# Which engine copies the probability tiles out of the matmul banks: from two engines to one, with the first output columns of two head pairs copied together

## The chip, the cores and the metric

The kernel runs on one core of a Trainium2 chip. The metric is the device time of one execution in microseconds (us). The kernel before took 426.64 us, the median of three runs (426.52, 426.64 and 428.88). The execution that was profiled took 426.48 us. Its trace spans 424.8 us, so 1.7 us lie outside of what the rows below can show.

## The reference

The inputs are q, k and v of shape 8 batches x 8 heads x 576 tokens x 64, and f, one forget value per batch, head and token. First comes a causal attention with a decay, then a small expert layer on the tokens of each batch with the highest scores:

```
scores = scale * q @ k^T                       # scale = 1/8
cum    = cumsum(log(clip(f, 1e-4, 1)))
scores = where(causal, -1e9, scores + cum_q - cum_k)
attn   = exp(scores - max);  attn = attn / (sum + 1e-9)
x      = (attn @ v), heads side by side        # 8 x 576 x 512
for each batch b:
    top = the 128 tokens with the highest x[b] @ w_gate
    xe  = x[b, top]
    out[b, top] = xe + sigmoid(xe @ w_gate) * (relu(xe @ w1) @ w2)
    out[b, others] = x[b, others]
```

Everything is float32. w1 is 512 x 1024 and w2 is 1024 x 512.

## The kernel before, in words

**Work by pairs of heads.** There are 32 pairs, four per batch. `pair_ops(p)` loads a pair's q and k and, per head, the decay row `e`, from which GpSimd cuts causal masks `m` (line 438). `pair_parts(p)` is the rest of a pair:

- TensorE computes the scores of the pair in four groups into PSUM banks (line 606). These matmuls use 64 rows of the array, since the heads are 64 wide, and two heads run side by side.
- VectorE adds mask or decay, writes the result to `p` and keeps the row minimum `nm` (line 650).
- ScalarE takes the exponential of `p` in place and sums the rows (line 698).
- TensorE transposes `p` in blocks of 64 columns into a pair of banks (line 717), in four groups: block row 3, then 1, 2 and 0.
- The transposed probabilities are copied from the banks into the tile `pt`, one copy per head and group. `copy_on` does it on ScalarE (line 351) or VectorE (line 355). The choice is the flag `other`: the second head's copy of the groups 2 and 3 goes to VectorE, all others to ScalarE. These two groups are the widest, 384 and 512 columns per head.
- TensorE multiplies `v` with `pt` (line 800; called the product below). The first 128 query columns of a pair go to one bank, the other 448 to a second. An even pair and the odd pair behind it share the first bank, side by side.
- The product is copied to a tile `ot` in two copies, 128 and 448 columns (line 351), transposed back (line 859), and VectorE scales it into `x` (line 864). `ot` has two buffers, so that a pair is turned back while the next is being copied.

**The expert layer by batches.** GpSimd forms the gate scores of a pair as soon as its `x` is there (lines 873, 877). With four pairs done, the scores of the batch are ranked on VectorE (line 1005), the 128 tokens gathered by DMA (line 1046), transposed (line 1068), multiplied with w1 (lines 1117, 1124) and w2 (lines 1170, 1178), and scattered back (line 1189). These matmuls use all 128 rows of the array; they are called MLP matmuls below. Each weight is split in two parts, high and low, for accuracy, mostly on GpSimd (lines 934, 937).

**What sets the order.** The program is not written in the order in which it runs. The class `Flow` is a planner: each step is added with the engine or engines that may do it, a cost, the steps it comes after, the buffers it takes and gives, and a number `place`. The planner then walks through modelled time and issues on each engine the ready step with the smallest place. The places are sums of constants (BD, PL, PM, PC and so on). Tokens named "ps" are the eight PSUM banks; others stand for tile buffers. For a step that either of two engines may do, BD is a handicap on VectorE, and with it the product's copies all went to ScalarE. Each engine executes its own instructions strictly in the order that the planner gave.

The functions that the diff touches:

Of the kernel before, what the change touches and what calls it, by code (L numbers as in the profile page):

```python
# [8 lines left out]
F32 = mybir.dt.float32  # L9
# [9 lines left out]
P = 128  # L19
# [12 lines left out]
class Flow:  # L32
# [16 lines left out]
           ("long", "full"): 0.02, ("full", "long"): 0.08,  # L49
           ("av", "row"): 0.15, ("av", "turn"): 0.13, ("av", "long"): 0.12, ("av", "full"): 0.1,  # L50
           ("row", "av"): 0.13, ("turn", "av"): 0.16, ("long", "av"): 0.2, ("full", "av"): 0.1}
# [127 lines left out]
def kernel(  # L179
# [32 lines left out]

    BD = 13.742
    WP = 17
    WQ = 0
    R0 = -128.692
    X0 = -110.557
    XE_ = -374.815
    XH_ = 10.943
    XM_ = -139.592  # L220
    XB_ = -7.064
    XN_ = -144.178
    XO_ = -217.739
    XU_ = 1.221
    XQ_ = 1037.015
    XR_ = 452.972
    XG_ = 100.433
    PL4 = -197.666
    GW = 62.808
    EPS = 0.124  # L230
    LOOK = 13
    PR = -556.913
    PL = -142.848
    PS = 1725.901
    PV = 96.032
    PM = -87.342
    PE_ = 464.517
    PC = -268.952
    PB = -64.844
    PD = -22.685  # L240
    VO = -0.967
    VD = 1
    GD = 0.1
    WS = -60.896
    WD = 742.816
    WL = 434.464
    RK = 76.029
    RD = -1.849
    XP = 18.421
    GO = 35.674  # L250
    GS = 0.497
    GL = 28.239
    LG = 2.69
# [49 lines left out]
    sgs = [const.tile([P, NCH], F32, name=f"sg{r}") for r in range(2)]  # L303

    vrs = [const.tile([P, NCH, P], F32, name=f"v{r}") for r in range(3)]
    ptb = [const.tile([P, 5 * 640], F32, name=f"pt{r}") for r in range(2)]
# [33 lines left out]
    def act(n):  # L340
        return {"act": n / 1200 + 0.05}
# [7 lines left out]
    def copy_on(e, d, s_):  # L349
# [4 lines left out]
        else:  # L354
            nc.vector.tensor_copy(d, s_)  # L355

    flow = Flow({"raw": 3, "rq": 3, "v": 3, "p0": 2, "p1": 2, "p4": 2, "pt": 2, "ot": 2,
                 "x": 2, "nm": 10, "h": 1, "hth": 1, "htl": 1, "xth": 1, "xtl": 1, "xe": 2, "srow": 1,
# [8 lines left out]
    z = {}  # L367
# [8 lines left out]
    def t_ones(e):  # L376
        z["ones"] = work.tile([P, S], F32, tag="ot", name="ones", bufs=2)
        nc.vector.memset(z["ones"], 1.0)
# [12 lines left out]

    tk_h, tk_ot, tk_srow = Token("h"), Token("ot", 3), Token("srow")
    tk_ep = Token("hth")
# [158 lines left out]
    NT = 4  # L552
    vts, pts, ots, xhs = {}, {}, {}, {}
    gates = {b: {"tk": Token("gs"), "done": []} for b in range(B)}
# [4 lines left out]
    def pair_parts(p):  # L559
# [148 lines left out]
        for i in (3, 1, 2, 0):  # L708
# [53 lines left out]
            for hh in range(2):  # L762
                other = hh == 1 and i >= 2
                if i == 0:
                    n_ = 4 * P - 2 * R * hh
                    x6 = add({"dve": n_ / 960 + 0.13} if other else {"act": n_ / 1200 + 0.1}, lambda e, cps=cps, hh=hh: cps(e, hh), after=[x5, d_rows],
                             place=t + PC + 0.01 * hh, give=[tk_t])
                else:
                    x6 = add(dve(2 * w) if other else act(2 * w), lambda e, cp=cp, hh=hh: cp(e, hh=hh), after=[x5, d_rows],
                             place=t + PC + 0.01 * hh, give=[tk_t])  # L770
                copied.append(x6)
# [5 lines left out]
        pieces = ((0, 1), (1, 1), (0, 0), (2, 1), (4, 1), (3, 1))  # L777
        tk_ot = Token("ot", 1)
        if odd:
            tk_av = [tails[p - 1], Token("ps")]  # L780
        else:

            tk_av = [Token("ps", 2), Token("ps")]
            tails[p] = tk_av[0]
        wdone = []
        avs = []
        for n, (j, g) in enumerate(pieces):
# [3 lines left out]
            def av(e, n=n, j=j, g=g, q0=q0, q1=q1):  # L791
                if j == 0:
                    avb[p, g] = bank(tk_av[g])
                if n == 0:
                    ots[p] = work.tile([P, S], F32, tag="ot", name=f"ot{p}", bufs=2)
                vt, pt = vts[p], pts[p]
                qo = SPL if odd and g == 0 else 0
                for par in range(2):
                    off = (640 * j if par == 0 else 2624 - 512 * j) + q0 - j * P
                    nc.tensor.matmul(  # L800
                        avb[p, g][par * D:(par + 1) * D, qo + q0 - g * SPL:qo + q1 - g * SPL],
                        vt[:, j, par * D:(par + 1) * D], pt[:, off:off + q1 - q0],
                        start=(j == 0), stop=(g == 0 or n == len(pieces) - 1))
# [3 lines left out]
        def av_all(e):  # L807
            for fn, _ in avs:
# [6 lines left out]
                 place=at + 0.01 * odd, take=[tk_ot] + tk_av[odd:], give=[tk_pt, tk_v], kind="av", lat=0.05)  # L815
        for g, w in ((0, SPL), (1, S - SPL)):
            def out(e, g=g, w=w):
                qo = SPL if odd and g == 0 else 0
                copy_on(e, ots[p][:, g * SPL:g * SPL + w], avb[p, g][:, qo:qo + w])

            avd[p] = x5
            wdone.append(add({**act(w), **dve(w)}, out, after=[x5], place=at + 0.2 + 0.3 * odd, give=[tk_av[g]]))

        rn = rns[b % 2][:, :, 2 * hp:2 * hp + 2]

# [26 lines left out]
        def back(e):  # L852
            ot = ots[p]
            tb = st["tb"] = pair(tk_b)
# [412 lines left out]
```

## Time and profile before

| | kernel before |
|---|---|
| median of three runs | 426.64 us |
| profiled execution, and its span | 426.48 us, 424.8 us |
| TensorE (PE) busy | 381.4 us, 90% |
| VectorE (DVE) busy | 307.7 us, 72% |
| ScalarE (ACT) busy | 306.7 us, 72% |
| GpSimd (POOL) busy | 262.9 us, 62% |
| VectorE's probability copies (line 355) | 64, 39.3 us |
| ScalarE's probability copies (line 351, into `pt`) | 256 |
| mean DMA rate | 162 GB/s |

Busy time is a share of the whole span, and the span has several stages: a short start, a stretch of attention alone, a long stretch in which attention and MLP matmuls mix, and an end with MLP matmuls alone. Which engine limits a stage must be read from that stage. A wait in the profile is idle time of an engine before an instruction, put down to what released it last.

### The profile page before, as it was taken

What the parts mean: (1) busy time and instruction counts of PE and PEld (TensorE: products, weight loads), DVE (VectorE), ACT (ScalarE), POOL (GpSimd) and SP (SyncE); (2) the same over time, 40 slices, a digit from 0 to 9 for tenths busy, and PEclk for the clock granted to TensorE, in tenths of its full rate; (3) what the DMA queues carried; (4) which work ended last, traced back from release to release, by engine and by line L of the source; (5) the groups of instructions that cost most, each with busy time, mean ns of one, the idle gap of its engine ahead of it and who ended that gap; (6) DMA issues with size and microseconds to landing.
All of it is one profiled execution on the core that took longest, in us unless ns stands there. A gap on an engine that the chain in (4) does not pass through costs nothing. (4 is left out here: it accounts for less than half of the span.)

```text
span 424.8 us, 11756 instructions
## 1 busy us (share of the span) xinstructions
PE 381.4 (90%) x3897; PEld 270.6 (64%) x3897; DVE 307.7 (72%) x1079; ACT 306.7 (72%) x961; POOL 262.9 (62%) x412
## 2 busy tenths in 40 slices
PE   2889998998979899989899999899989999999995
PEld 1546656566556657566576767668576766868873
DVE  5658758785989899869696976978689685825421
ACT  2887999898898998766787777966888767513220
POOL 5585779997959889766483665547574654134201
PEclk9898999999999999999999999999999999999999
DMA  7798977876979787563576637726674423011101
GB/s 167 198 235 208 258 212 222 228 225 169 282 175 249 200 234 220 169 176 104 157 193 168 183 113 198 232 70 175 206 193 131 139 60 95 17 50 57 49 2 49
DMA packets 77155, 68.67 MB, mean 162 GB/s; under 512 B 47747, under 2 KB 56998, under 8 KB 77094
## 3 DMA queue, kind: packets, MB, share of 16 engines
q1 hardware_dynamic: 75654, 63.43, 54.5%
q0 software_dynamic: 1280, 4.20, 3.1%
q8 instruction: 31, 0.51, 0.6%
q14 instruction: 30, 0.25, 0.2%
q10 hardware_dynamic: 160, 0.30, 0.2%
HBM read 56.18 MB, written 11.70 MB: 160 GB/s over the span
## 5 line engine op out<-in xcount | busy, mean ns | idle before, releaser
L698 ACT ACTIVATE p<-p,nm 128x448 f32<-128x448 f32 (+4 forms) x288 | 165.9, 582 | 9.9 <-DVE nm L650 9.6
L438 POOL TENSOR_SCALAR_AFFINE_SELECT m<-e 128x320 f32<-128x320 f32 (+3 forms) x256 | 114.3, 476 | 45.5 <-DMA e<-eq 16.4
L606 PE MATMUL banks<-rk,rq 64*128 64x192 f32 (+4 forms) x768 | 120.5, 427 | 13.0 <-DMA rq<-in_qk_dram 8.4
L351 ACT COPY pt<-banks 128x256 f32<-128x256 f32 (+4 forms) x256 | 91.2, 400 | 21.6 <-DVE pt L355 10.0
L650 DVE CUSTOM_DVE_ANT_0 p<-banks,m 128x320 f32<-128x320 f32 (+3 forms) x256 | 100.6, 418 | 6.7 <-PE banks L606 3.5
L606 PEld LDWEIGHTS banks<-rk,rq 64*128 64x128 f32 x768 | 74.3, 193 | 34.3 <-DVE nm L650 9.8
L800 PE MATMUL banks<-pt,v 128*64 128x448 f32 (+4 forms) x768 | 91.7, 391 | 0.2
L717 PE MATMUL banks<-ident,p 64*128 64x64 f32 x1472 | 69.6, 226 | 15.5 <-DVE pt L355 9.9
L717 PEld LDWEIGHTS banks<-ident,p 64*128 64x128 f32 x1472 | 61.8, 139 | 27.3 <-DVE pt L355 14.3
L800 PEld LDWEIGHTS banks<-pt,v 128*64 128x64 f32 x768 | 48.1, 137 | 45.5 <-issue 29.9
L355 DVE COPY pt<-banks 128x512 f32<-128x512 f32 x64 | 39.3, 622 | 27.8 <-ACT pt L351 20.5
L873 POOL TENSOR_TENSOR gj<-x,wg 128x640 f32<-128x640 f32 x24 | 37.4, 1558 | 33.3 <-DVE x L864 33.1
L698 ACT ACTIVATION_READ_ACCUMULATOR p<-p,nm 128x1 f32 x288 | 55.6, 193 | 0.0
L864 DVE TENSOR_TENSOR x<-banks,rn 128x640 f32<-128x640 f32 x32 | 26.3, 820 | 25.6 <-PE banks L859 24.5
L351 ACT COPY ot<-banks 128x128 f32<-128x128 f32 x64 | 22.4, 404 | 30.2 <-PE banks L800 29.8
L877 POOL TENSOR_TENSOR acc<-acc,gj 128x640 f32<-128x640 f32 x24 | 38.3, 1596 | 1.6
L1005 DVE SCALAR_TENSOR_TENSOR j<-srow,sg,later 128x576 uint8<-128x576 f32 (+1 forms) x40 | 35.9, 898 | 0.7
L1189 POOL DMA_INDIRECT out_dram<-xe,idx x8 | 8.6, 1080 | 43.9 <-DVE xe L1185 27.5
L650 DVE CUSTOM_DVE_ANT_0 p<-banks,e 128x384 f32<-128x384 f32 x64 | 34.7, 548 | 0.4
L650 DVE CUSTOM_DVE_ANT_0 p<-banks,m,nm 128x192 f32<-128x192 f32 x64 | 26.6, 415 | 8.4 <-ACT p L698 2.7
L650 DVE DVE_READ_ACCUMULATOR2_ANT nm<- 128x1 f32 (+1 forms) x384 | 31.0, 81 | 0.0
L1170 PE MATMUL banks<-w2h,hth 128*128 128x512 f32 x64 | 25.9, 405 | 0.5 <-ACT hth L1150 0.3
(83 smaller groups left out, 415.9 us busy)
## 6 DMA issues: line engine op xcount, KB each, us to landing
e<-eq SPq DMA_DIRECT2D x62, 288.0 KB
rk<-in_qk_dram SPq DMA_DIRECT2D x32, 288.0 KB
out_dram<-x SPq DMA_DIRECT2D x16, 512.0 KB
rq<-in_qk_dram SPq DMA_DIRECT2D x32, 144.0 KB
rq<-in_qk_dram SPq DMA_DIRECT2D x32, 128.0 KB
v<-in_v_dram SPq DMA_DIRECT2D x32, 128.0 KB
v<-in_v_dram SPq DMA_DIRECT2D x32, 80.0 KB
srow<-sd SPq DMA_DIRECT2D x7, 320.0 KB
```

Source lines behind the costliest of these rows:

```text
L351: nc.scalar.copy(d, s_)
L355: nc.vector.tensor_copy(d, s_)
L438: nc.gpsimd.affine_select(out=dst, in_=src, pattern=w, compare_op=ALU.is_ge, fill=NEG, base=base, channel_multiplier=1)
L606: nc.tensor.matmul(st["sc", u][hh][:, o:o + k1 - k0], q_rows(raws["q", p], hh, i), raws["k", p][rows, k0:k1], start=True, stop=True)
L650: nc.vector.tensor_tensor_reduce(out=into(hh, i, r_, x0, x1), in0=blocks(b_[r_, x0 - k0:x1 - k0], hh, i), in1=blocks(in1(), hh, i), scale= ...
L698: nc.scalar.activation(x, x, AF.Exp, bias=st["nm", hh, i], scale=-1.0, accum_out=l)
L717: nc.tensor.transpose(tp[:, g, col:col + R], src, ident[g * R:g * R + R, g * R:g * R + R])
L800: nc.tensor.matmul(avb[p, g][par * D:(par + 1) * D, qo + q0 - g * SPL:qo + q1 - g * SPL], vt[:, j, par * D:(par + 1) * D], pt[:, off:off + ...
L864: nc.vector.tensor_tensor(out=xhs[key][:, :, w_ * P:(w_ + 1) * P].rearrange("p c (h d) -> p c h d", h=2), in0=st["tb"][:, :, 0:NCH * D].re ...
L873: nc.gpsimd.tensor_tensor(out=gj if hp else acc, in0=xhs[key][:, :, w0:w1], in1=wg[:, hb * HB + w0:hb * HB + w1].unsqueeze(1).broadcast_to ...
L877: nc.gpsimd.tensor_tensor(out=acc, in0=acc, in1=gj, op=ALU.add)
L1005: nc.vector.scalar_tensor_tensor(junk[0:n, :], st["srow"][0:n, 0:S], sg()[0:n, c:c + 1], later[0:n, o:o + S], ALU.subtract, ALU.is_gt, acc ...
```

## The change

Five things are different.

- `other` is always false: the 64 probability copies of VectorE are ScalarE's now.
- The two output buffers become one tile `both`, 128 x 2 x 576, one half for even pairs and one for odd.
- The 448 columns of each pair are still copied after that pair's product. The first 128 columns of an even pair are no longer copied on their own: after the odd pair's product one copy takes both pairs' columns from the shared bank (`heads`).
- The rest of a pair (`back_parts`: row sums, turning back, scaling, gate) is added after that joint copy for both pairs, so an even pair is turned back only when the odd pair's product is there.
- The planner has a cost between two products in a row, ("av", "av"), and nearly all its constants have new values, so that nearly every engine's instructions stand in another order.

```diff
-           ("av", "row"): 0.15, ("av", "turn"): 0.13, ("av", "long"): 0.12, ("av", "full"): 0.1,
+           ("av", "row"): 0.15, ("av", "turn"): 0.13, ("av", "long"): 0.12, ("av", "full"): 0.1, ("av", "av"): 0.15,
...
-    BD = 13.742
+    BD = 17.003
...
-    EPS = 0.124
+    EPS = 0.061
...
+    both = const.tile([P, 2, S], F32, name="both")
...
-    flow = Flow({"raw": 3, "rq": 3, "v": 3, "p0": 2, "p1": 2, "p4": 2, "pt": 2, "ot": 2,
+    flow = Flow({"raw": 3, "rq": 3, "v": 3, "p0": 2, "p1": 2, "p4": 2, "pt": 2, "ot0": 1, "ot1": 1,
...
-                other = hh == 1 and i >= 2
+                other = False
...
-        tk_ot = Token("ot", 1)
+        tk_ot = Token(f"ot{odd}")
...
-            tk_av = [Token("ps", 2), Token("ps")]
+            tk_av = [Token("ps"), Token("ps")]
...
-        for g, w in ((0, SPL), (1, S - SPL)):
-            def out(e, g=g, w=w):
-                qo = SPL if odd and g == 0 else 0
-                copy_on(e, ots[p][:, g * SPL:g * SPL + w], avb[p, g][:, qo:qo + w])
-
-            avd[p] = x5
-            wdone.append(add({**act(w), **dve(w)}, out, after=[x5], place=at + 0.2 + 0.3 * odd, give=[tk_av[g]]))
-
+        def out(e):
+            copy_on(e, both[:, odd, SPL:S], avb[p, 1][:, 0:S - SPL])
+
+        def heads(e):
+            copy_on(e, both[:, :, 0:SPL], avb[p, 0][:, 0:2 * SPL].rearrange("p (g x) -> p g x", g=2))
+
+        avd[p] = x5
+        wdone.append(add(act(S - SPL), out, after=[x5], place=at + 0.2 + 0.3 * odd, give=[tk_av[1]]))
+        if odd:
+            x5 = add(act(2 * SPL), heads, after=[x5], place=at + 0.2 + 0.3 * odd, give=[tk_av[0]])
+            rests[p - 1](x5)
+            back_parts(p, st, wdone, at, sums, d_l, tk_ot, x5)
+        else:
+            rests[p] = lambda x: back_parts(p, st, wdone, at, sums, d_l, tk_ot, x)
+
+    def back_parts(p, st, wdone, at, sums, d_l, tk_ot, joint):
+        b, hp = divmod(p, NP)
+        odd = p % 2
+        wdone = wdone + [joint]
...
-            ot = ots[p]
+            ot = both[:, odd, :]
```

How the change moves instructions is shown at three places. The first is ScalarE's order around the copies of pair 13 (`pt1` is the probability tile of odd pairs, `p13` and `p14` hold the exponentials of pairs 13 and 14, `nm` their row minima). Before:

```order
L698 ACTIVATE p13_2_2271,st1_100<-p13_2_2271,nm13_3_1_2483 128x192
L351 COPY pt1_114<-banks_78 128x4x128
L351 COPY pt1_114<-banks_78 128x2x128 x2
L698 ACTIVATE p14_0_2460,st2_101<-p14_0_2460,nm14_0_0_2485 128x576
L351 COPY pt1_114<-banks_78 128x3x128
```

And now:

```order
L352 COPY pt1_115<-banks_78 128x4x128 x2
L699 ACTIVATE p13_2_2350,st1_100<-p13_2_2350,nm13_3_1_2421 128x192
L352 COPY pt1_115<-banks_78 128x2x128 x2
L699 ACTIVATE p14_0_2529,st2_101<-p14_0_2529,nm14_0_0_2549 128x576
L352 COPY pt1_115<-banks_78 128x3x128 x2
```

The 128x4x128 and 128x3x128 copies, of which ScalarE had one each, stand there twice in a row. Over the whole program ScalarE's probability copies go from 256 to 320 and VectorE's from 64 to none.

The second place is ScalarE's order around the output copies of pairs 10 and 11. Before:

```order
L351 COPY ot10_2284<-banks_78 128x128
L351 COPY ot10_2284<-banks_78 128x448
L698 ACTIVATE p40_97,st0_99<-p40_97,nm12_3_0_2251 128x64
L698 ACTIVATE p12_2_2217,st0_99<-p12_2_2217,nm12_3_1_2269 128x192
L698 ACTIVATE p13_0_2244,st1_100<-p13_0_2244,nm13_0_1_2343 128x576
L351 COPY ot11_2323<-banks_78 128x128
L351 COPY ot11_2323<-banks_78 128x448
```

And now, from pair 11's copies on (pair 10's 128x448 stands 17 rows higher):

```order
L352 COPY pt0_114<-banks_78 128x2x128 x2
L352 COPY both_110<-banks_78 128x448
L352 COPY both_110<-banks_78 128x2x128
L699 ACTIVATE p13_2_2350,st1_100<-p13_2_2350,nm13_3_0_2412 128x192
L699 ACTIVATE p13_0_2297,st1_100<-p13_0_2297,nm13_1_1_2360 128x320
```

One 128x2x128 copy stands where each pair had its own 128x128.

The third place is TensorE's order where the MLP matmuls begin (`xth0` is the first batch's gathered tokens, `w1h` and `w1l` the two parts of w1). Before, with the products of pairs 12 and 13 just ahead of these rows:

```order
L717 MATMUL banks_78<-ident_81,p14_0_2460 128x64
L606 MATMUL banks_78<-rk15_2260,rq0_86 128x64 x2
L606 MATMUL banks_78<-rk15_2260,rq0_86 128x192 x2
L606 MATMUL banks_78<-rk16_2556,rq1_87 128x384 x2
L606 MATMUL banks_78<-rk16_2556,rq1_87 128x192 x2
L606 MATMUL banks_78<-rk16_2556,rq1_87 128x320 x2
L717 MATMUL banks_78<-ident_81,p15_0_2597 128x64 x24
L1117 MATMUL banks_78<-w1h_115,xth0_0_2759 128x512
L1117 MATMUL banks_78<-w1l_116,xth0_0_2759 128x512
L1117 MATMUL banks_78<-w1h_115,xth0_0_2759 128x512
L1117 MATMUL banks_78<-w1l_116,xth0_0_2759 128x512
```

And now, with pair 10's product just ahead:

```order
L607 MATMUL banks_78<-rk13_1866,rq1_87 128x384 x2
L1127 MATMUL banks_78<-w1h_116,xth0_0_2292 128x512
L1127 MATMUL banks_78<-w1l_117,xth0_0_2292 128x512
L607 MATMUL banks_78<-rk13_1866,rq1_87 128x192 x2
L607 MATMUL banks_78<-rk13_1866,rq1_87 128x320 x2
L718 MATMUL banks_78<-ident_81,p12_0_2087 128x64 x16
L607 MATMUL banks_78<-rk13_1866,rq1_87 128x448 x2
L799 MATMUL banks_78<-pt1_115,v2_113 64x448 x4
```

The first MLP matmul comes after 11 products instead of 14, and the MLP matmuls stand in pieces between attention steps instead of in one block. Counted over the whole program, TensorE's order passes from steps with a 64-row contraction (scores, transposes of `p` and of outputs) to steps that use 128 rows (MLP matmuls, products, index steps) 33 times before and 58 times now. The number of its instructions is the same. The first 27 rows of SP's queue (its loads) are the same, and so is TensorE's order behind the product of pair 31, but for the turns back of pairs 30 and 31 and the last batch's score rows, which stand a few MLP matmuls later.

## Rows read from the trace of the kernel before

**Rows 1.** The page, part 1: busy us (share of the span) xinstructions

```profile
PE 381.4 (90%) x3897; PEld 270.6 (64%) x3897; DVE 307.7 (72%) x1079; ACT 306.7 (72%) x961; POOL 262.9 (62%) x412
```

**Rows 2.** Windows: stretch, its length, busy time of each engine, granted clock, DMA

```profile
20.00:140.00 120.00, 107.45 (x1278) 71.43 (x1275) 93.13 (x364) 106.66 (x353) 96.78 (x151) 0.98 0.81 223
134.00:164.00 30.00, 26.91 (x367) 18.82 (x363) 26.76 (x90) 26.65 (x91) 26.32 (x38) 1.00 0.78 198
164.00:375.00 211.00, 198.41 (x2037) 143.16 (x2038) 163.86 (x566) 156.79 (x493) 121.91 (x185) 1.00 0.52 148
```

**Rows 3.** Waits: who waited for whom, total us, times, longest us

```profile
DVE pt L355 <- ACT pt L351: 20.5, 29, 3.0
...
ACT pt L351 <- DVE pt L355: 10.0, 18, 1.0
PE banks L717 <- DVE pt L355: 9.9, 15, 1.3
...
PE banks L859 <- ACT ot L351: 5.0, 7, 0.9
...
PE banks L717 <- ACT pt L351: 2.6, 5, 1.2
```

**Rows 4.** Lines by shape, ScalarE: busy us, mean ns, idle before

```profile
L351 ACT COPY pt<-banks 128x256 f32<-128x256 f32 x96 | 32.6, 377 | 3.2 <-PE banks L717 2.7
...
L351 ACT COPY pt<-banks 128x512 f32<-128x512 f32 x32 | 18.8, 588 | 5.8 <-PE banks L717 4.2 <-DVE pt L355 1.5
...
L351 ACT COPY pt<-banks 128x384 f32<-128x384 f32 x32 | 15.5, 484 | 10.0 <-DVE pt L355 8.5 <-PE banks L717 1.5
...
L351 ACT COPY ot<-banks 128x128 f32<-128x128 f32 x32 | 8.5, 266 | 29.8 <-PE banks L800 29.8
```

**Rows 5.** Lines by shape, VectorE: the probability copies

```profile
L355 DVE COPY pt<-banks 128x512 f32<-128x512 f32 x32 | 22.1, 691 | 17.0 <-ACT pt L351 14.3 <-PE banks L717 2.7
L355 DVE COPY pt<-banks 128x384 f32<-128x384 f32 x32 | 17.7, 553 | 10.8 <-ACT pt L351 6.2 <-PE banks L717 4.3
```

**Rows 6.** Windows of line 355 alone: stretch, length, VectorE busy (x instructions)

```profile
20.00:140.00 120.00, 14.86 (x24) 0.98 0.81 223
```

**Rows 7.** Timeline of all engines from 105.5: start, length, engine, line, operation

```profile
105.82 1.11 ACT L351 COPY pt<-banks 128x512 f32<-128x512 f32 x3
...
106.42 0.69 DVE L355 COPY pt<-banks 128x512 f32<-128x512 f32 x1 [0.34 <-ACT pt L351]
...
107.16 0.14 PEld L717 LDWEIGHTS banks<-ident,p 64*128 64x128 f32 x2 [0.73 <-DVE pt L355]
```

**Rows 8.** Timeline of TensorE, 128 to 166, the last stretch without MLP matmuls

```profile
131.67 5.62 PE L800 MATMUL banks<-pt,v 128*64 128x448 f32 x48
...
150.60 5.62 PE L800 MATMUL banks<-pt,v 128*64 128x448 f32 x48
...
163.96 0.50 PE L1117 MATMUL banks<-w1h,xth 128*128 128x512 f32 x1
164.29 0.39 PE L1117 MATMUL banks<-w1l,xth 128*128 128x512 f32 x1
```

**Rows 9.** Timeline of TensorE, 183 to 200

```profile
195.58 1.20 PE L1178 MATMUL banks<-w2h,htl 128*128 128x512 f32 x4 [0.42 <-DVE g L1089]
196.71 1.34 PE L717 MATMUL banks<-ident,p 64*128 64x64 f32 x36
```

**Rows 10.** Timeline of TensorE, the end

```profile
404.60 0.46 PE L1068 MATMUL banks<-ident,xe 64*128 64x64 f32 x8
...
406.04 0.39 PE L1117 MATMUL banks<-w1h,xth 128*128 128x512 f32 x1
...
411.50 1.07 PE L1178 MATMUL banks<-w2h,htl 128*128 128x512 f32 x4
412.41 1.03 PE L1143 MATMUL banks<-ident,h 128*128 128x128 f32 x8
```

More of the change, by code (lines that the diff above doesn't have):

```diff
@@ L211 @@
     FR = 3 * R
-    BD = 13.742
+    BD = 17.003
     WP = 17
     WQ = 0
[L216 to L229, printed above, removed]
-    EPS = 0.124
-    LOOK = 13
[L232 to L241, printed above, removed]
+    R0 = -112.531
+    X0 = -80.055
+    XE_ = -435.953
+    XH_ = 35.944
+    XM_ = -269.256
+    XB_ = -6.162
+    XN_ = -260.971
+    XO_ = -297.011
+    XU_ = 1.451
+    XQ_ = 887.605
+    XR_ = 440.833
+    XG_ = 122.837
+    PL4 = -306.718
+    GW = 70.696
+    EPS = 0.061
+    LOOK = 13
+    PR = -444.931
+    PL = -62.883
+    PS = 1660.693
+    PV = 149.607
+    PM = -69.055
+    PE_ = 360.879
+    PC = -267.606
+    PB = -34.433
+    PD = -18.932
+    VO = -1.905
     VD = 1
     GD = 0.1
[L244 to L252, printed above, removed]
+    WS = -90.032
+    WD = 727.705
+    WL = 447.716
+    RK = 69.243
+    RD = -2.401
+    XP = 25.102
+    GO = 33.367
+    GS = 0.817
+    GL = 22.573
     LG = 2.69
@@ L376, in t_ones @@
     def t_ones(e):
-        z["ones"] = work.tile([P, S], F32, tag="ot", name="ones", bufs=2)
+        z["ones"] = both[:, 0, :]
         nc.vector.memset(z["ones"], 1.0)
@@ L390, in t_ec @@
         nc.vector.tensor_scalar(z["ec"], z["cum"], -8.0, None, ALU.mult)
-    tk_h, tk_ot, tk_srow = Token("h"), Token("ot", 3), Token("srow")
+    tk_h, tk_ot, tk_srow = Token("h"), Token("ot0", 3), Token("srow")
     tk_ep = Token("hth")
@@ L552 @@
     NT = 4
-    vts, pts, ots, xhs = {}, {}, {}, {}
+    vts, pts, xhs, rests = {}, {}, {}, {}
     gates = {b: {"tk": Token("gs"), "done": []} for b in range(B)}
@@ L793, in av @@
                     avb[p, g] = bank(tk_av[g])
-                if n == 0:
-                    ots[p] = work.tile([P, S], F32, tag="ot", name=f"ot{p}", bufs=2)
                 vt, pt = vts[p], pts[p]
```

## The prediction, made before the changed kernel was run

> **What bounds the kernel now.** I read the busy times first. TensorE is busy for 381.4 us of 424.8, VectorE and ScalarE for about 307 each [rows 1]. So TensorE is nearest to its limit, and a change that leaves its work alone can only win or lose its idle time, 43.4 us in all, or change what it costs to pass from one kind of step to another. The windows tell where that idle time lies [rows 2]. From 20 to 140, where there is attention alone, TensorE is busy for 107.45 of 120 and ScalarE for 106.66: two engines at 89%, each with about 13 us to spare. From 164 to 375, with MLP matmuls mixed in, TensorE has 198.41 of 211, ScalarE only 156.79. There TensorE alone sets the pace. The attention stretch moves two pairs in 18.93 us (products at 131.67 and 150.60 [rows 8]).
>
> The waits come next [rows 3]. TensorE's transposes wait 9.9 us, 15 times, for a copy on VectorE to free their banks, 2.6 us for copies on ScalarE, and its turns back 5.0 us for output copies. VectorE's own copies stand waiting for ScalarE's copies for 20.5 us, ScalarE's for VectorE's for 10.0 us: the two write the same tile and go one behind the other. The timeline shows such a pair of copies [rows 7]: ScalarE's 128x512 copy starts at 105.82, VectorE waits 0.34 us and starts at 106.42, and the weight load of the next transposes has waited 0.73 us when the copy releases it at 107.16.
>
> **The change, part by part.** The sum is made against the profiled 426.48 us, 0.16 below the median of 426.64.
>
> *Copies leave VectorE.* 32 of 691 ns and 32 of 553 ns go, 39.8 us with their 27.8 us of idle time in front [rows 5]. VectorE is not the limit (307.7 of 424.8), so this counts only through who waits for it. On ScalarE such copies take 588 and 484 ns [rows 4], so the second of a pair ends a little over 0.1 us earlier, and the hand-over falls away; in exchange it stands in a fuller queue. Of the 9.9 us of TensorE's waits I take half as gained: **-5.0**. The ends are 0 (each wait is replaced by one for ScalarE) and -9.9.
>
> *ScalarE's load.* It gets 32 x 588 + 32 x 484 ns = 34.3 us more. The joint copy takes 377 ns by the row of 128x256, instead of 2 x 266 [rows 4]: 16 x 155 ns = 2.5 us less. In sum 306.7 + 31.8 = 338.5, 80% of the span. What matters is the attention stretch. Of the 64 copies 24 lie there, 14.86 us on VectorE [rows 6]; at ScalarE's durations, 12 of each width, they are 12.9, less 6 x 0.155 for the joint copies: 106.66 + 12.0 = 118.7 of 120. That would be full. It is a little less in fact, since copies in a row overlap (the three at 105.82 take 1.11 us together [rows 7], their durations of 588, 377 and 377 add to 1.34), and a third of ScalarE's 10.0 us of waits for VectorE, 3.3, should lie in this stretch and go. If only that gives way, the stretch grows by 12.0 - 3.3 = 8.7; if its other 10 us of idle time closes too, by 0. Since TensorE has as much slack there as ScalarE, and VectorE delivers its minima sooner, I take **+1.5**.
>
> A rule speaks against this step. The Trainium skill, page "TensorEngine Tiling (Array Packing)", section "PSUM Bottleneck", says that where tiling has made the matmuls quick, copies out of PSUM may become the limit, and to use both ScalarE and VectorE for them. By that rule the term would be the upper end, +8.7, and the change a loss; the windows, with 54 us of ScalarE's time free behind 164, bear it out for the first stretch alone.
>
> *MLP matmuls three pairs earlier.* They begin after 11 products instead of 14. Before, they start at 163.96 [rows 8]; from 134 to 164 TensorE is idle for 3.1 us of 30 [rows 2], and now there is work to lay in. I take **-2.5** (ends 0 and -3.1).
>
> *MLP matmuls in pieces.* From 164 to 375 TensorE is idle for 12.6 us [rows 2]. About half of the 9.9 us is part of it and already counted; of the other 8 or so I take a third as filled by pieces: **-2.5** (ends 0 and -8).
>
> *More passages.* TensorE passes from 64-row to 128-row steps 58 times instead of 33. The price: four MLP matmuls inside a block take 0.91 us from start to start (411.50 to 412.41 [rows 10]), four that stand alone between a wait and transposes 1.13 (195.58 to 196.71 [rows 9]), 0.22 more for going in and out. At the first passage, 163.96, the first matmul takes 0.33 to the second's start [rows 8], 0.10 more than the usual 0.23, which agrees. 25 x 0.22 = **+5.5**. The ends are 0, if every piece lies in time that was idle, and 12.5, if each costs a whole first matmul of 0.50.
>
> *The joint copy.* An even pair's turn back now waits for the odd pair's product. Behind it stand scaling and gate, which have most of a pair's time to spare; the token of `both` is given back before the next even product, a pair later. I cost it at nothing, with what that rests on: an odd pair's product, copy and turns back keep ahead of the next even pair's. Its cost without that cover is the third rival.
>
> *Start and end.* SP's first loads are the same, and the first matmul waits for them. At the end the last batch's gathered tokens are transposed at 404.60 and needed at 406.04 [rows 10]: 1.4 us of slack take the later turns back of pairs 30 and 31, about one copy of 0.54 and two MLP matmuls. Both at 0.
>
> Sum: -5.0 + 1.5 - 2.5 - 2.5 + 5.5 = -3.0, so **423.5 us**, 0.7% below the median. That is within the 1% (4.3 us) that a measurement of this kernel can tell from no change.
>
> **The rivals.** *VectorE's copies were the whole trouble.* All of the 9.9 and 3.1 go, the filling gives 2.5, and half of the passages fall into idle time (+2.75): 426.5 - 12.75 = 413.7. For it: VectorE loses 67 us of copies and waits, and minima, ranks and scaling all come sooner. Against: the copies still come one after the other.
>
> *ScalarE becomes the bound of the attention stretch.* It stands in the place of VectorE in the waits (0 instead of -5.0), its stretch grows by 8.7, passages cost 5.5, and only the -5.0 of the two MLP terms and half a gain of 2.5 remain: 426.5 + 6.7 = 433.2. It decides where ScalarE's share from 20 to 140 passes about 95% and exponentials queue behind copies. For it: 118.7 of 120. Against: the MLP matmuls now start inside that stretch, so a slow ScalarE no longer leaves TensorE without work.
>
> *The joint copy holds up the turns back.* TensorE already waits 5.0 us for output copies [rows 3]. Each of 16 times the odd product is followed by a 448 copy and a joint one, and turns back for two pairs behind them. If half of these cost 0.6 us, that is 4.8 more: 428.3.
>
> That the copies don't move can be left out: the order has none on VectorE.
>
> **How the numbers follow.** Forecast 0.42, its own range 419 to 428; VectorE the whole trouble 0.28; ScalarE the bound 0.20; joint copy 0.10. Faster by over 1% means below 422.4: all of the second and a quarter of the first, 0.39. Slower by over 1% means above 430.9: nearly all of the third case and little of others, 0.20. The rest, 0.41, is within 1%. With a tenth left out on each side the range is 414 to 434.
>
> **What would show it.** VectorE's busy time near 268 and no copy of `pt` on it. ScalarE's near 335, and its share from 20 to 140 above 95%: if TensorE's idle time in that stretch stays near 12, my +1.5 holds; if it grows beyond 18, the second rival does. TensorE's waits of transposes for copies in sum near 7.5 instead of 12.5. The first MLP matmul near 140. TensorE's busy time up by some 4 to 6 for the passages; if it stays at 381, that term was too large. Turns back waiting much more than 5.0 would be the third rival. I am wrong altogether if the time is far from 423.5 and TensorE's idle time and passages don't account for it, for instance by a later start or a gap at the end.

## The result, and the profile after

The changed kernel takes 413.79 us, the median of four runs (412.55 to 415.16); the kernel before took 426.72 in the same comparison (426.52 to 428.88). The ratio is 0.9687, with a 95% interval from 0.9643 to 0.973: 3.1% faster. The forecast was 423.5, and the range ended at 414, just above the measured time. The number of the first rival, 413.7, came out, though its mechanism accounts for a part only, as the experiments show.

The profiled execution took 413.60 us, its span is 411.9. Part 1 of the page, busy us (share of the span) xinstructions, answers to [rows 1]:

```profile
PE 384.9 (93%) x3897; PEld 269.0 (65%) x3897; DVE 269.5 (65%) x1015; ACT 328.4 (80%) x1009; POOL 260.6 (63%) x412
```

TensorE's busy time rose by 3.5 us, and its idle time fell from 424.8 - 381.4 = 43.4 to 411.9 - 384.9 = 27.0, by 16.4. The span fell by 12.9, the difference of the two. So the whole gain is idle time of TensorE. The windows say where it was. First the kernel before, in three stretches that [rows 2] do not have (length, busy time of PE, PEld, DVE, ACT, POOL with their instructions, granted clock, DMA share, GB/s):

```profile
8.40:31.00 22.60, 19.23 (x166) 12.34 (x168) 15.28 (x56) 18.19 (x53) 13.13 (x26) 0.92 0.82 208
31.00:140.00 109.00, 98.41 (x1164) 65.88 (x1161) 87.24 (x338) 97.09 (x321) 88.24 (x137) 0.98 0.80 220
140.00:375.00 235.00, 219.59 (x2318) 158.15 (x2314) 184.96 (x641) 178.48 (x565) 143.35 (x216) 1.00 0.55 154
```

The same stretches of the changed kernel, and two that answer to [rows 2]:

```profile
8.40:31.00 22.60, 19.43 (x164) 13.74 (x166) 14.41 (x55) 19.22 (x54) 13.96 (x28) 0.85 0.78 220
20.00:140.00 120.00, 112.54 (x1281) 73.41 (x1281) 82.86 (x348) 114.46 (x372) 100.04 (x156) 0.96 0.83 225
31.00:140.00 109.00, 102.06 (x1169) 66.43 (x1167) 77.27 (x322) 104.42 (x340) 90.73 (x140) 0.97 0.82 222
...
164.00:375.00 211.00, 209.41 (x2167) 148.96 (x2166) 140.91 (x539) 174.66 (x536) 123.67 (x187) 1.00 0.53 152
140.00:375.00 235.00, 232.09 (x2422) 164.03 (x2418) 160.32 (x598) 195.44 (x601) 145.32 (x215) 1.00 0.55 157
```

TensorE's idle time from 31 to 140 goes from 10.59 to 6.94, from 140 to 375 from 15.41 to 2.91. These are 3.65 and 12.50, nearly all of the 16.4. From 8.4 to 31, and in what lies outside 8.4 to 375, next to nothing changed (3.4 and 3.2; 14.0 in both). From 164 to 375 TensorE is busy for 209.41 of 211 us. In that stretch only 1.6 us of waits are left that another order could remove. (A busy TensorE is not TensorE at its peak: its matmuls overlap in the trace, so short stalls can lie inside busy time.)

Its waits (who waited for whom, total us, times, longest us), against [rows 3]:

```profile
PE banks L607 <- DMA rq<-in_qk_dram: 8.3, 1, 8.3
PE banks L718 <- ACT pt L352: 3.4, 6, 0.8
PE banks L607 <- DVE nm L651: 3.0, 4, 1.4
PE banks L869 <- ACT pt L352: 0.9, 4, 0.2
```

The 8.3 us are the first load, 8.4 before. The transposes' waits for copies went from 9.9 + 2.6 to 3.4, those of the turns back from 5.0 to 0.9. The timeline of TensorE shows what stands in their place (start, us, operation), where [rows 8] had no MLP matmul before 163.96. The first one now starts at 131.64; I had expected it near 140:

```profile
130.72 0.98 PE L607 MATMUL banks<-rk,rq 64*128 64x384 f32 x4
131.64 0.50 PE L1127 MATMUL banks<-w1h,xth 128*128 128x512 f32 x1
131.97 0.40 PE L1127 MATMUL banks<-w1l,xth 128*128 128x512 f32 x1
132.40 1.13 PE L607 MATMUL banks<-rk,rq 64*128 64x192 f32 x8
133.37 0.66 PE L718 MATMUL banks<-ident,p 64*128 64x64 f32 x16
133.86 0.97 PE L607 MATMUL banks<-rk,rq 64*128 64x448 f32 x4
134.76 2.92 PE L799 MATMUL banks<-pt,v 128*64 128x448 f32 x24
...
138.62 0.50 PE L1127 MATMUL banks<-w1h,xth 128*128 128x512 f32 x1
138.95 0.40 PE L1127 MATMUL banks<-w1l,xth 128*128 128x512 f32 x1
139.19 0.39 PE L1127 MATMUL banks<-w1h,xth 128*128 128x512 f32 x1
139.42 0.40 PE L1127 MATMUL banks<-w1l,xth 128*128 128x512 f32 x1
139.74 0.59 PE L718 MATMUL banks<-ident,p 64*128 64x64 f32 x12
```

Every row begins before the one above it has ended (matmuls are pipelined) or within 0.03 us of it, and no row shows a wait before it. Compare a stretch of the kernel before in mid-program, in which blocks of MLP matmuls leave gaps at the attention steps behind them (in brackets the idle time before a row, and its releaser):

```profile
235.60 0.86 PE L717 MATMUL banks<-ident,p 64*128 64x64 f32 x20
236.86 0.46 PE L717 MATMUL banks<-ident,p 64*128 64x64 f32 x7 [0.40 <-DVE pt L355]
...
240.72 0.66 PE L1143 MATMUL banks<-ident,h 128*128 128x128 f32 x4 [0.60 <-DVE nm L650]
241.13 0.47 PE L1170 MATMUL banks<-w2h,hth 128*128 128x512 f32 x1
...
247.74 0.27 PE L960 MATMUL banks<-ident,sg 128*5 128x128 f32 x1 [0.55 <-DVE sg L880]
```

### The profile page after: what moved, and what is told of

Same layout as the page of the kernel before. It is cut to its first block, busy times and chain, and to the rows that moved or that the text cites. A ratio compares the mean times of both kernels' runs of the same rounds, so it can differ in the third digit from the quotient of the medians.

```text
span 411.9 us, 11754 instructions
## 1 busy us (share of the span) xinstructions
PE 384.9 (93%) x3897; PEld 269.0 (65%) x3897; DVE 269.5 (65%) x1015; ACT 328.4 (80%) x1009; POOL 260.6 (63%) x412
## 5 line engine op out<-in xcount | busy, mean ns | idle before, releaser
L699 ACT ACTIVATE p<-p,nm 128x576 f32<-128x576 f32 (+4 forms) x288 | 166.2, 585 | 4.7 <-DVE nm L651 2.6
L439 POOL TENSOR_SCALAR_AFFINE_SELECT m<-e 128x384 f32<-128x384 f32 (+3 forms) x256 | 112.4, 469 | 74.5 <-DVE nm L651 36.5
L607 PE MATMUL banks<-rk,rq 64*128 64x192 f32 (+4 forms) x768 | 122.8, 426 | 12.3 <-DMA rq<-in_qk_dram 8.3
L352 ACT COPY pt<-banks 64x256 f32<-64x256 f32 (+3 forms) x320 | 118.2, 433 | 13.3 <-PE banks L718 11.5
L718 PE MATMUL banks<-ident,p 64*128 64x64 f32 x1472 | 72.3, 231 | 6.2 <-ACT pt L352 3.4
L799 PEld LDWEIGHTS banks<-pt,v 128*64 128x64 f32 x768 | 45.6, 137 | 49.1 <-issue 31.8
L1015 DVE SCALAR_TENSOR_TENSOR j<-srow,sg,later 128x576 uint8<-128x576 f32 (+1 forms) x40 | 37.5, 938 | 0.6
L352 ACT COPY both<-banks 128x448 f32<-128x448 f32 (+1 forms) x48 | 22.1, 479 | 16.4 <-PE banks L799 16.2
L651 DVE CUSTOM_DVE_ANT_0 p<-banks,m,nm 128x192 f32<-128x192 f32 x64 | 26.5, 414 | 10.3 <-POOL m L439 5.1
L1164 DVE TENSOR_TENSOR htl<-banks,hth 128x512 fp32r<-128x512 f32 x16 | 10.8, 678 | 27.2 <-ACT hth L1160 27.2
L1127 PE MATMUL banks<-w1h,xth 128*128 128x512 f32 x64 | 26.4, 413 | 0.1
```

What stands on the lines that cost most here:

```text
L352: nc.scalar.copy(d, s_)
L439: nc.gpsimd.affine_select(out=dst, in_=src, pattern=w, compare_op=ALU.is_ge, fill=NEG, base=base, channel_multiplier=1)
L607: nc.tensor.matmul(st["sc", u][hh][:, o:o + k1 - k0], q_rows(raws["q", p], hh, i), raws["k", p][rows, k0:k1], start=True, stop=True)
L651: nc.vector.tensor_tensor_reduce(out=into(hh, i, r_, x0, x1), in0=blocks(b_[r_, x0 - k0:x1 - k0], hh, i), in1=blocks(in1(), hh, i), scale= ...
L699: nc.scalar.activation(x, x, AF.Exp, bias=st["nm", hh, i], scale=-1.0, accum_out=l)
L718: nc.tensor.transpose(tp[:, g, col:col + R], src, ident[g * R:g * R + R, g * R:g * R + R])
```

## The experiments

Two theories stood at first. **A**, the first rival's mechanism: what counts is that VectorE's copies are gone. **B**: what counts is the new order of TensorE's work. B has two forms: in B1 the new constants are better by themselves; in B2 they are better only with the changed structure. Later came **F**, that the gain is a fit of one order, which a small change of a constant loses, against **S**, that the structure carries it and it stands such changes. Ratios are to the kernel before on the same chip (medians 426.3 to 427.0), with 95% intervals.

**The engine of the copies, with the order held.** The planner's choice and model stay; only the engine that executes the 64 copies is another. In the changed kernel they go to VectorE:

```diff
- lambda e, cp=cp, hh=hh: cp(e, hh=hh)
+ lambda e, cp=cp, hh=hh, i=i: cp("dve" if hh == 1 and i >= 2 else e, hh=hh)
```

> The changed kernel with its plan untouched (all orders of TensorE, GpSimd and SP the same row for row), but the 64 second copies of groups 2 and 3 are executed by VectorE again, each at the point where the plan had it on ScalarE. Theory A (VectorE's copies and the waits on them were what cost the time): most of the gain goes, 423 to 427 us, with transposes waiting for VectorE's copies 8 us or more. Theory B (the new order of TensorE's work, which fills its idle time with MLP pieces, is what won, and the engine of the copies hardly matters): 414 to 418 us, TensorE's idle time from 164 to 375 still under 5 us.

Measured: 419.15 us, 0.9821 [0.9793, 0.9848]. That lies between the two ranges, nearer to B's. Part 1 of its page, and three of TensorE's waits:

```profile
PE 384.2 (92%) x3897; PEld 268.5 (64%) x3897; DVE 300.0 (72%) x1079; ACT 306.5 (73%) x945; POOL 259.2 (62%) x412
...
PE banks L718 <- DVE pt L356: 3.6, 5, 1.1
...
PE banks L607 <- DVE pt L356: 2.3, 3, 1.6
PE banks L869 <- DVE pt L356: 1.9, 4, 0.5
```

TensorE is idle for 417.3 - 384.2 = 33.1 us, 10.3 less than in the kernel before, although VectorE makes the same 64 copies. Its transposes wait 3.6 us for VectorE's copies and 0.4 for ScalarE's, where it was 9.9 and 2.6. In the kernel before the copies go to ScalarE (`cp("act", hh=hh)`):

> The kernel before with its plan untouched (TensorE, GpSimd, SP the same row for row), but VectorE's 64 copies are executed by ScalarE at the point where the plan had them on VectorE. Theory A: a good part of the gain comes alone from this, 415 to 421 us. Theory B: TensorE's order still leaves its idle time in place, 424 to 430 us; ScalarE's share from 20 to 140 above 95% and a longer attention stretch.

Measured: 429.32, 1.0062 [1.004, 1.0084], as B expected, but ScalarE's share from 20 to 140 is 92% (110.95 of 120), not above 95%. TensorE's waits in this second kernel:

```profile
PE banks L717 <- ACT pt L351: 9.6, 17, 1.0
...
PE banks L606 <- ACT pt L351: 5.5, 14, 1.0
PE banks L859 <- ACT ot L351: 5.2, 8, 0.9
```

The transposes wait 9.6 us for ScalarE where they waited 9.9 + 2.6 for both engines, the scores 5.5 where it was 1.2, the turns back 5.2 where it was 5.0. That is the lower end of my first term: a wait for ScalarE in the place of each wait for VectorE. In the changed order the same edit is worth 419.15 - 413.79 = 5.4 us; in the order before it costs 2.4. A as the main cause falls: the order with VectorE's copies in it already keeps 7.7 of the 13 us. B alone doesn't hold either, since in the changed order the engine of the copies is worth the other 5.4.

**VectorE's load without the copies.** The changed kernel with 64 reductions more on VectorE, for which nothing waits, placed where its copies would stand:

```diff
+ nc.vector.tensor_reduce(out=junkd[:, 0:i + 1], in_=ident.unsqueeze(1).broadcast_to([P, i + 1, P]),
+                         axis=mybir.AxisListType.X, op=ALU.add)
```

> The changed kernel with its plan untouched, plus 64 reductions on VectorE of 512 and 384 columns of a constant tile, about as long as the 64 copies that it lost, each where the plan copies the second head's half. Nothing waits for them and they wait for nothing. Theory A1 (VectorE's load itself, some 40 us, was the cost): 419 us or more. Theory A2 (the coupling was the cost: copies of one tile by two engines that wait for each other, in order): 413 to 416 us, although VectorE is as busy as before the change. Theory B: also 413 to 416 us; it is told from A2 by the run with VectorE's copies in the changed order.

Measured: 417.77 (four runs from 415.91 to 419.59), 0.9794 [0.9757, 0.9831], between the range of A1 and that of A2 and B. The group of the added work (line, xcount | busy, mean ns):

```profile
L360 DVE TENSOR_REDUCE junkd<-ident 128x4 f32<-128x512 f32 x64 | 38.8, 607 | 0.1
```

38.8 us of mere load (VectorE's busy time rises by 30.5 us, to 300.0) cost 4.0 us. So of the 5.4 us above, about 4 can be VectorE's load alone, which delays its other results: TensorE now waits 1.6 us for VectorE's `oh`, where it was 0.2. What the hand-over between the two engines that write one tile costs beside it stays open, since the kernel above also has 64 copies less on ScalarE and this one hasn't.

**The parts, planned anew.** The change has three parts: C, the copies on ScalarE (`other = False`); J, the joint copy with `both` and `back_parts`; N, the new constants with ("av", "av"). Each combination is the one kernel with the lines of the other, and the planner makes a new order for each.

> The kernel before with other = False and nothing else: its old constants, but the planner makes a new plan that knows the copies are ScalarE's. The order has 59 passages from 64-row to 128-row steps instead of 33, and MLP matmuls begin after 12 products instead of 14. Theory A: 415 to 420 us. Theory B (the new constants are what won): 424 to 432 us, since the old constants were fitted to the other split of the copies.

> The kernel before with the new constants and the new cost between two products, and nothing else: VectorE keeps its 64 copies, each pair its own output copies. Passages 56, first MLP matmul after 12 products. Theory B1 (the new constants alone make the better order, whatever the copies): 415 to 420 us. Theory B2 (constants and structure belong together, the order is only good where it was fitted): 424 to 432 us. Theory A (the copies): 424 us or more as well, with transposes waiting for VectorE's copies some 10 us.

> The kernel before with the new constants and all probability copies on ScalarE: the change without the joint copy. Passages 77. Theory J (the joint copy and the turns back of both pairs in a row are a needed part): 420 us or more. Without it, by B1 and by A: 413 to 417 us. B2: 422 us or more, since the order is a new one again.

> The changed kernel with the old constants and without the cost between two products: copies on ScalarE and joint copy, planned by the old places. Passages 58, first MLP matmul after 11 products. B1 (constants): 423 to 430 us, as for the kernel before with its copies moved. A or J (structure): 414 to 419 us.

> The changed kernel with the second head's copies of groups 2 and 3 given back to VectorE and planned so: joint copy and new constants stay. Passages 56, first MLP matmul after 14 products. By the run with VectorE's copies in the changed order, which took 419.2 us, a fitting plan should give 416 to 421 us (B1); B2 says 423 us or more, as the order is new.

> The joint copy alone: the changed kernel with the old constants and with VectorE's 64 copies given back to it. Passages 65. It is the last corner of the three parts. From the other corners (old constants: 426.9 without either part, 425.7 with ScalarE's copies, 422.5 with both) the joint copy should bring about 3 us: 423 to 426 us, if parts add up. If an order only fits by luck (theory F): 428 us or more.

| parts | median us | ratio to before | TensorE busy, idle, us (profiled run) |
|---|---|---|---|
| none | 426.9 | 1 | 381.4, 43.4 |
| C | 425.69 | 0.9979 [0.9955, 1.0003] | 389.7, 34.0 |
| J | 435.14 | 1.0228 [1.0169, 1.0288] | 393.2, 40.5 |
| N | 445.00 | 1.0436 [1.0383, 1.049] | 391.8, 47.1 |
| C + J | 422.52 | 0.989 [0.9856, 0.9923] | 385.2, 34.9 |
| C + N | 429.31 | 1.0061 [1.0037, 1.0084] | 391.2, 36.6 |
| J + N | 429.45 | 1.0051 [1.0034, 1.0068] | 394.0, 34.4 |
| C + J + N | 413.79 | 0.9687 [0.9643, 0.973] | 384.9, 27.0 |

The new constants alone lose 4.4% (four runs from 440.65 us at a granted clock of 0.984 to 447.15 at 0.958). B1 falls, and the expectations that rested on it missed: 445.00, 429.31 and 429.45 lie above their ranges. For C + J, 422.52 lies between the two ranges; for J, 435.14 is far from the 423 to 426 of parts that add up. No part by itself gains 1%. Only C + J with the old constants, and all three together, are clearly faster. Of B2 one half stands: the new constants are better only in this structure. The other half does not: the old constants, too, do better with C + J (422.5) than in the structure they came from (426.9).

The last column shows a second thing that an order sets. TensorE's instructions are the same 3897 in all eight kernels, yet it is busy for 381.4 to 394.0 us. C, C + N and J + N remove 7 to 9 us of its idle time and lose about as much or more in busy time (8.3, 9.8 and 12.6). The two faster kernels add less than 4. The clock is not the main reason, since the profiled runs of all kernels but the one before have mean granted clocks of 0.980 to 0.988. Nor is it the number of passages: J + N has 56, C 59 and the changed kernel 58. What lengthens the busy time stays open.

**How close the fit is.** One constant, EPS, is raised by a tenth in each kernel (0.061 to 0.067; 0.124 to 0.136), and in the changed kernel again GW goes from 70.696 to 74.0. The new EPS makes other orders (76 passages instead of 58, 43 instead of 33), the new GW nearly the same one (59 instead of 58):

> The changed kernel with one constant moved by a tenth, EPS 0.067 instead of 0.061, so that the planner makes another order (passages 76 instead of 58, first MLP matmul after 12 products) from the same structure. Theory F (the gain is the fit of one order, found by trying): 419 to 427 us, most of the gain gone. Theory S (the structure, copies on ScalarE and joint copy, lets nearly any order run well): 412 to 418 us.

> The kernel before with EPS 0.136 instead of 0.124, the same relative step (passages 43 instead of 33, first MLP matmul after 12 products). Theory F: 430 to 442 us, as the order before was fitted too. Theory S: 424 to 430 us.

> The changed kernel with GW 74.0 instead of 70.696, which moves only a few of TensorE's rows (passages 59 instead of 58, first MLP matmul after 11 products). If the gain hangs on the order as a whole and not on each row of it, 412 to 418 us. If even this breaks it, as the tenth on EPS did, 420 us or more.

The changed kernel with the other EPS took 430.01 to 438.34 us (median 437.27), above even F's range. Its granted clock differed between the runs, 0.962 to 0.985. The best of them is 16 us above the changed kernel at about the same clock (0.983). The kernel before with the other EPS took 434.49, 1.02 [1.016, 1.024], as F expected. With the other GW it is 414.63, 0.9726 [0.9705, 0.9747], which the interval doesn't part from the changed kernel. So F holds for both kernels, with a limit: the gain hangs on the order as a whole, and a nearly equal order keeps it.

The trace of the EPS kernel is of its slowest execution, 438.34 us at a clock of 0.971, so it can't tell where the 430.01 us went. In it TensorE is idle for 38.7 us and busy for 397.9, both more than in the changed kernel (27.0 and 384.9). Its largest waits beside the first load:

```profile
PE banks L1180 <- DVE nm L651: 4.2, 2, 3.5
PE banks L970 <- DVE sg L890: 3.9, 1, 3.9
...
PE banks L799 <- DVE nm L651: 2.8, 1, 2.8
```

Nearly all of it is three single stalls, the longest 3.9 us, in which the step at the head of TensorE's queue isn't ready. Each was followed by more lost time. From 162.0 to 165.4, behind the longest, the granted clock is 0.51, near the lower of its two levels (1.2 and 2.4 GHz), and a product of 24 matmuls takes 4.39 us, where one takes 2.92 in the changed kernel at 134.76. Timeline of TensorE, 156 to 168:

```profile
162.02 0.37 PE L970 MATMUL banks<-ident,sg 128*5 128x128 f32 x1 [3.87 <-DVE sg L890]
162.32 4.39 PE L799 MATMUL banks<-pt,v 128*64 128x448 f32 x24
```

Behind the other two, from 189.0 to 192.4 and from 268.0 to 271.4, the clock is 0.53 and 0.54.

**The joint copy.** The changed order, with the joint copy executed on VectorE, and with it made as two copies:

```diff
- copy_on(e, both[:, :, 0:SPL], avb[p, 0][:, 0:2 * SPL].rearrange("p (g x) -> p g x", g=2))
+ for g in range(2):
+     copy_on(e, both[:, g, 0:SPL], avb[p, 0][:, g * SPL:(g + 1) * SPL])
```

> The changed kernel with its plan untouched, but the 16 joint copies of the first 128 columns are executed by VectorE at the point where the plan had them on ScalarE. If ScalarE's load limits the changed kernel (95% from 20 to 140, 80% in all), 6 us less of it and VectorE at 65% should give 411 to 413 us. If a hand-over from ScalarE to VectorE costs more than the copy's time, as the run with VectorE's probability copies suggests, 414 to 417 us.

> The changed kernel with its plan untouched, but the joint copy is done as two copies of 128 columns, one for each pair, at the same point: ScalarE has 16 instructions more. If the joining itself saves time, 2.5 us of ScalarE's come back, up to 416 us. If the joining matters only through the plan it allowed, no change: 412.5 to 415 us.

Measured: 415.45, 0.9742 [0.9703, 0.978] on VectorE; 413.86, 0.9699 [0.9677, 0.972] as two copies. Joining the copies is worth nothing in itself, and the engine of the joint copy makes no difference that the intervals show. What J gives it gives through the plan that it allows, among other things another place for the turns back; which of them counts was not tested.

**The price of a passage.** 128 small matmuls that add zeros (each stands in the trace as two instructions) are put between the two MLP matmuls of each w1h, w1l and w2h, w2l couple: in one kernel with a contraction of 64 rows, in the other of 128, so that their difference is the passage out of 128-row work and back.

```diff
+ nc.tensor.matmul(q["hp", n][0:nr, 0:R], zz[0:R, 0:1].broadcast_to([R, nr]), ident[0:R, 0:R], start=False, stop=False)
```

> The changed kernel with its plan untouched, and in each of the 128 steps of the MLP that multiply with the high and the low part of a weight, between the two, one small matmul of 64 columns with a contraction of 64 rows that adds zeros. Each makes TensorE pass to 64-row work and back. If a passage costs 0.22 us, as the forecast read from the trace, this kernel is 28 us slower than the one with 128-row insertions, some 440 to 455 us; if a passage costs about 0.1 or less, 13 us or less.

> The same insertions with a contraction of 128 rows, so that no passage is added: the control for the run with 64 rows. 128 small matmuls of 0.1 us or so each: 420 to 432 us.

Measured: 483.41, 1.1325 [1.1303, 1.1347] with 64 rows, 441.51, 1.0343 [1.0318, 1.0367] with 128. Both are above what was expected: even the insertion without a passage costs 27.7 us, 0.22 for each. The difference of the two is 41.9 us, 0.33 for each, where 28 was expected. The timelines agree; with 64 rows:

```profile
421.51 0.39 PE L1186 MATMUL banks<-w2h,hth 128*128 128x512 f32 x1
421.82 0.43 PE L1185 MATMUL banks<-ident,zz 64*128 64x64 f32 x2
422.19 0.50 PE L1186 MATMUL banks<-w2l,hth 128*128 128x512 f32 x1
422.52 0.40 PE L1186 MATMUL banks<-w2h,hth 128*128 128x512 f32 x1
```

and with 128:

```profile
392.66 0.40 PE L1186 MATMUL banks<-w2h,hth 128*128 128x512 f32 x1
392.89 0.33 PE L1185 MATMUL banks<-ident,zz 128*128 128x64 f32 x2
393.03 0.48 PE L1186 MATMUL banks<-w2l,hth 128*128 128x512 f32 x1
393.35 0.40 PE L1186 MATMUL banks<-w2h,hth 128*128 128x512 f32 x1
```

From one w2h matmul to the next it is 1.01 us against 0.69.

## Why the prediction was wrong, by its steps

**What bounds the kernel: right.** TensorE's work is the floor, and only its idle time and its passages could change. The gain is 16.4 us less idle time, with 3.5 more busy.

**Waits, MLP earlier, MLP in pieces: the failed step.** These three terms stood at -5.0, -2.5 and -2.5; with the +1.5 for ScalarE they made 8.5 us less idle time, and it was 16.4. The first experiment parts them. With VectorE's copies put back in the changed order, idle time is 10.3 us below the kernel before: that is the order's, where the two MLP terms had 5.0. Moving the copies takes off the other 6.1 us (33.1 to 27.0), where the first term and ScalarE's load had 3.5 together. The sentence that failed most is "of the other 8 or so I take a third as filled by pieces", and with it the half of the 9.9. I cost each wait of [rows 3] by itself, as if what filled one left the others. But the order alone took the transposes' waits for copies from 12.5 us to 4.0, with the copies still on two engines, while scores and turns back took over 4.2 us of waits for VectorE (2.3 + 1.9). And from 140 to 375 the changed kernel's idle time is 2.91 us instead of 15.41. My upper ends (9.9, 3.1 and 8) add to 21.0 and held the truth; the values between were the mistake. That the waits go because TensorE's queue holds an MLP piece or a score step where a copy or a minimum would be late is how I read the timeline; no run shows it by itself.

How much of this comes from the earlier start and how much from the pieces stays open, since each new plan moves both. Nor are the two, as far as they can be counted, the whole: C + J with the old constants has as many passages (58) and as early a start (11 products) as the changed kernel, and takes 422.5.

**The first rival: its number, not its cause.** Its conditions, all of 9.9 and 3.1 gone, nearly came true. But they did not come from the engine of the copies alone: with the order held, that edit gave a loss of 2.4 us in the one order and a gain of 5.4 in the other, about 4 of them for VectorE's mere load. That the number fits is luck.

**ScalarE's load: +1.5 not seen as a loss.** Its share from 20 to 140 reached 95% (114.46 of 120), the point that I named, and TensorE's idle time there did not grow beyond 18: it fell from 12.55 to 7.46. ScalarE's busy time is 328.4 where I expected about 335, since copies in a row overlap (the groups of copies into `pt` add up to 127.4 us by their own durations and cover 118.2). The rule of the Trainium skill, page "TensorEngine Tiling (Array Packing)", section "PSUM Bottleneck", to use both engines for copies out of PSUM, is not borne out in this order: the copies on two engines are 5.4 us slower in the first experiment. In the order before it is, by 2.4.

**Passages: the price too low, the sum too high.** In the insertion the price is 0.33 us, where I took 0.22. In the pieces of the changed kernel it is nearer to mine: four MLP matmuls from 138.62 to the transposes at 139.74 take 1.12 us, 0.21 above the 0.91 of [rows 10]. Yet TensorE's busy time rose by 3.5, not 5.5, and part of that is the clock. Behind waits of 0.36 and 0.93 us that end at 115.57 and 116.93, the granted clock fell to about half (window from 118 to 125, the clock third from the end):

```profile
118.00:125.00 7.00, 7.00 (x70) 4.92 (x69) 5.15 (x20) 4.78 (x16) 6.64 (x8) 0.51 0.59 137
```

Ahead of 31 us, too, the mean clock is 0.85 instead of 0.92. The kernel with the other GW has 59 passages, 0.92 ahead of 31 and 1.00 from 31 to 140, and is busy for 382.7, only 1.3 more than the kernel before. By these two, as an estimate, such passages cost some 1 to 3.5 us in all, and the term was too large. Why it is less than 25 times 0.21 stays open.

**Joint copy, start and end at nothing: right.** Two copies take the same time as one; the turns back wait 0.9 us instead of 5.0, so the third rival is out; and outside 8.4 to 375 TensorE is idle for 14.0 us in both.

**Chances.** I gave 0.41 to "within 1%" and 0.39 to faster. The chance of 0.28 for the rival was all that reached the outcome, and the lower end of the range should have been nearer to the sum of the upper gains, 426.5 - 21.0 + 5.5 = 411.

## What to carry to other kernels

Where a planner or a table sets the order, judge the idle time of the engine that bounds the kernel as a whole: an order that nearly always has a ready piece of independent work at the head of that engine's queue can remove most short waits at once, more than wait-by-wait costing tells. Look at the engine's busy time as well: most of the orders here that cut idle time paid it back there. To price a single edit, hold the order fixed and change only who executes it; a new plan mixes the edit with the fit. Before crediting a structure with a gain, move one constant of the order a little and see how far the order itself moves: here a tenth on one of them cost 2% in the one kernel and more than the whole gain in the other, while a step that hardly moved the order cost nothing measurable.

## What the runs showed of the hardware

- A 64-row matmul between 128-row ones costs 0.33 us more than a 128-row one of the same width in the same place (41.9 us over 128 of them).
- 38.8 us of instructions on an engine that is 65% busy, for whose result nobody waits, still cost 4.0 us: other results of that engine came later (TensorE's waits for `oh` went from 0.2 to 1.6 us).
- TensorE's granted clock fell to its lower level behind some waits: to 0.51 after 3.87 us of idle time in the EPS kernel, with 4.39 us for a product that takes 2.92 otherwise, and to 0.51 behind waits of 0.36 and 0.93 us in the changed kernel. It does not follow each wait: the kernel before waits 1.26 us before 145.56, and its mean clock from 40 to 375 is 1.00.
- The mean clock of a whole execution did not order the times of the changed kernel: 412.55 us (granted clock 1.000), 413.60 (0.983), 413.98 (0.983) and 415.16 (0.997). With the new constants alone it did: 440.65 (0.984), 443.23 (0.972), 446.77 and 447.15 (both 0.958).
